# Attention products, value products and projections as 64x32 tiles on two row halves, with a new written order

## The chip, the cores and the metric

The kernel runs on one core of a Trainium2 chip. The metric is the device time of the program in microseconds. Engines are named as in the profile: PE (TensorE; PEld is its weight loads), ACT (ScalarE), DVE (VectorE), POOL (GpSimd) and SP (SyncE, which issues most DMAs).

## The reference

One input x (1 x 2048 x 512, bf16) goes through two attention layers of 32 heads of 16 each, and the two results are mixed by a gate:

```
g = sigmoid((x * gate_w).sum(-1, keepdims=True))

A:  q, k, v = heads of x @ wqkv
    pq = q @ w_phi ; pk = k @ w_phi                       (per head, 16 x 16)
    phi_q = [softmax(pq), softmax(-pq)] ; phi_k likewise
    kv = phi_k^T v ; z = sum over positions of phi_k
    o = (phi_q kv) / (phi_q z + 1e-6) ;  a = o @ wo

B:  q, k, v = heads of x @ wqkv
    p = softmax(q k^T / 4) ;  b = (p v) @ wo

out = g * a + (1 - g) * b
```

Layer B is the large part: 32 heads x 2048 x 2048 scores. Layer A is linear in the length.

## The kernel before, in words

**Blocks and tiles of layer B.** The 32 heads lie in four rows of eight (a row is the 128 partitions of a projected q or k). A block `b` of 32 is one row, one chunk of 512 queries and one parity, that is four heads: head `i` of the block sits in partitions 32i to 32i + 31 of `kT_B` (keys) and `qz` (queries; the other head of the same 32 partitions is zeroed in `qz`, of which there is one copy for each parity). A tile is (block, head i, key tile kt): 128 keys x 512 queries of scores, 64 tiles a block, 2048 in all.

**Scores.** `qk_mm` (line 1007) makes a tile with one matmul, contraction 32, 128 output columns: a row tile 32x128 of the array. Four heads have four row tiles, which may run side by side, each into a PSUM bank of its own. The order of heads over a block rotates.

**Two ways to an exponential.** 1272 tiles go in pairs (a slot) through ScalarE: `add_qk`, then `add_exp` (line 1131) exponentiates 128x1024 out of two neighbouring banks into `Ebuf`. The other 776 tiles (`DN` per block, in 202 groups of up to four) go through VectorE: `add_group` (line 1082) makes the tile (operation `dq`) and `D1` (line 1100, or 1090 for two tiles at once) turns scores into the bits of a bf16 exponential by an addition and a conversion to int16. GpSimd then adds constants to those bits (`shifted`, line 1076), twice, which gives two more terms of an approximation of the exponential.

**Value products.** `pv_mm` (line 1147) multiplies the exponentials of a tile with `vaug` (values and a column of ones): contraction 128, 32 output columns, so four heads are four column tiles 128x32 of the array, all adding into the one bank `psO` (`add_pv` for slots, `add_pvd` for the groups, whose tiles are multiplied three times, once for each term). At the end of a block VectorE copies `psO` out, and DMAs move the sums of the row of ones so that they can divide.

**Projections.** `columns` (line 765) does 128 x 512 outputs as four column tiles 128x32; `fill` (line 771) makes an operation of each contraction step, and `drain` the copy out of PSUM. The products with 128x128 or 128x64 weights (values, row sums of layer A, its kv and numerators) keep the whole array.

**What sets the order.** Nothing is scheduled on the chip. `Plan.add` records operations with what they read and write. `TABLE` holds, for each engine, the written order of the operations' numbers; `homes` gives the PSUM bank of each operation that opens one; `pairs` names the tiles that `D1` takes two at a time. `Plan.place` puts the lists together and adds what each operation waits for; `Plan.emit` (line 534) turns this into waits on one counting semaphore for each engine: each operation's last instruction raises its engine's count by one, and an engine waits until another's count is reached. An engine's own earlier operations are not waited for on PE. PE takes its instructions in the written order, so an operation that waits holds up all that stand behind it. PSUM has eight banks: six for slots, the same six and a seventh (`M`) for groups and fills, and one for `psO`.

```
def qk_mm(e, t, bank, half=None):
    b, i, kt = t
    cols = slice(0, NQ) if half is None else slice(256 * half, 256 * (half + 1))
    return e.matmul(bank, lhsT=kT_B[32 * i:32 * i + 32, ROW[b // 2] % 2, 128 * kt:128 * (kt + 1)],
                    rhs=qz[32 * i:32 * i + 32, b // 2 % 4, b % 2, cols], start=True, stop=True,
                    tile_position=(32 * i, 0))
```

## Time and profile before

| | |
|---|---|
| timed runs | 654.52 and 656.64 us, median 655.58 |
| profiled execution: span from first to last instruction | 653.1 us |
| busy in it: PE, PEld | 646.6, 229.7 us |
| busy in it: DVE, ACT, POOL | 615.8, 626.6, 420.4 us |
| TensorE clock granted | 1.000 |

The profile gives the span of the profiled execution; its own time lies beside it only as the timed runs do, 1.4 and 3.5 us above the span. PE's busy time runs from a matmul's start to its modelled end, and matmuls overlap, so 99% does not say that the array streams all the time: the distance from start to start does. The lines of `columns` (767), `qk_mm` (1010) and `pv_mm` (1152) are helpers' lines; they stand for many operations.

### The profile page before, as it was taken

To read this page: it belongs to the slowest core of one execution; us is meant where nothing else is said; L and a number is where in the kernel's file an instruction comes from. 1 tells how busy PE (TensorE), PEld (TensorE's weight loads), DVE (VectorE), ACT (ScalarE), POOL (GpSimd) and SP (SyncE) were. 2 spreads that over 40 slices of the span, in tenths; PEclk is the share of its full clock that TensorE was granted. 3 is DMA by queue.
4 is the path that set the end of the run, shared out by engine and by line. 5 is a ranking of instruction groups with operands and counts; after the bars stand their busy time and mean duration, and the time that the engine had idled before them with its cause. 6 is when DMAs were issued, how large, how long until landed. Compare 5 with 4: busy or idle time off the path is not lost.

```text
span 653.1 us, 20595 instructions
## 1 busy us (share of the span) xinstructions
PE 646.6 (99%) x8771; PEld 229.7 (35%) x8771; DVE 615.8 (94%) x1013; ACT 626.6 (96%) x710; POOL 420.4 (64%) x445
## 2 busy tenths in 40 slices
PE   9999999999999999999999999999999999999998
PEld 5332333433333333333333243333233234333333
DVE  6999899999999789999999999999999989999993
ACT  5999999899999999999999999989999999998996
POOL 7475567565657625676567777766875675577682
PEclk9999999999999999999999999999999999999999
DMA  7530101000010000100113331313201323035121
GB/s 131 116 90 20 24 13 29 11 11 21 10 29 10 19 12 11 26 13 6 29 39 92 63 99 48 78 34 82 52 23 49 85 53 96 33 82 111 29 58 59
DMA packets 67948, 30.95 MB, mean 47 GB/s; under 512 B 53208, under 2 KB 62808, under 8 KB 67856
## 3 DMA queue, kind: packets, MB, share of 16 engines
q1 hardware_dynamic: 65840, 28.82, 18.7%
q8 instruction: 69, 1.13, 0.7%
q10 hardware_dynamic: 1632, 0.79, 0.5%
q14 instruction: 23, 0.19, 0.1%
q0 software_dynamic: 384, 0.02, 0.1%
HBM read 7.87 MB, written 8.88 MB: 26 GB/s over the span
## 4 chain that ended last, share of the span: by engine, by line
PE 85%; ACT 10%; DVE 4%; issue 0%; DVEq 0%
PE psO L1152 32%; PE psS L1010 30%; PE psS L767 15%; ACT E_t L1131 10%; PE psS L1433 2%; PE psS L868 1%; PE psS L855 1%; DVE Tx_t L1100 1%; PE psS L1530 1%; DVE Ty_t L1100 1%; PE psS L1517 1%; PE psS L718 1%; DVE vA_t L1100 1%; DVE Wp_t L1100 0%; PE psS L1392 0%; PE psS L1473 0%
## 5 line engine op out<-in xcount | busy, mean ns | idle before, releaser
L1131 ACT ACTIVATE E_t<-psS 128x1024 bf16<-128x1024 f32 x633 | 592.4, 1059 | 15.3 <-PE psS L1010 14.5
L1010 PE MATMUL psS<-qz_t,kTB_t 32*128 32x512 bf16 (+1 forms) x2054 | 265.7, 384 | 2.0 <-ACT E_t L1120 0.6
L1100 DVE TENSOR_SCALAR Tx_t<-psS 128x512 int16<-128x512 f32 x268 | 175.3, 680 | 3.5 <-PE psS L1010 2.7
L1010 PEld LDWEIGHTS psS<-qz_t,kTB_t 32*128 32x128 bf16 x2054 | 72.9, 91 | 224.2 <-ACT E_t L1131 112.5
L1152 PE MATMUL psO<-E_t,vaug_t 128*32 128x512 bf16 x1272 | 124.4, 385 | 0.0
L1100 DVE TENSOR_SCALAR Ty_t<-psS 128x512 int16<-128x512 f32 x122 | 81.2, 683 | 5.5 <-PE psS L1010 5.2
L1076 POOL INT64_ADD vA_t<-vA_t x68 | 68.6, 1014 | 19.4 <-PE psO L1152 19.0
L1152 PE MATMUL psO<-vA_t,vaug_t 128*32 128x512 bf16 x534 | 53.1, 385 | 0.0
L1100 DVE TENSOR_SCALAR Tz_t<-psS 128x512 int16<-128x512 f32 x74 | 49.0, 681 | 2.5 <-PE psS L1010 2.0
L1076 POOL INT64_ADD Ty_t<-Ty_t x43 | 43.3, 1008 | 10.1 <-PE psO L1152 9.0
L1152 PEld LDWEIGHTS psO<-E_t,vaug_t 128*32 128x32 bf16 x1272 | 32.4, 95 | 42.8 <-issue 33.5
L1100 DVE TENSOR_SCALAR oT_t<-psS 128x512 int16<-128x512 f32 x66 | 43.9, 682 | 3.2 <-PE psS L1010 2.4
L1152 PE MATMUL psO<-Ty_t,vaug_t 128*32 128x512 bf16 (+1 forms) x450 | 45.9, 385 | 0.0
L1100 DVE TENSOR_SCALAR vA_t<-psS 128x512 int16<-128x512 f32 x66 | 44.1, 681 | 0.9 <-PE psS L1010 0.7
L1100 DVE TENSOR_SCALAR WAT_t<-psS 128x512 int16<-128x512 f32 x66 | 43.8, 680 | 0.4 <-PE psS L1010 0.4
L767 PE MATMUL psS<-Wp_t,xT_t 128*32 128x512 bf16 x512 | 41.2, 382 | 0.0
L767 PE MATMUL psS<-xT_t,WB_t 128*32 128x512 bf16 x480 | 39.1, 383 | 0.0
L1100 DVE TENSOR_SCALAR Wp_t<-psS 128x512 int16<-128x512 f32 x56 | 37.5, 681 | 0.5 <-PE psS L1010 0.5
L1076 POOL INT64_ADD phiQT_t<-Tx_t x19 | 19.3, 1015 | 22.9 <-DVE Tx_t L1100 20.7
L1076 POOL INT64_ADD Ty_t<-Tx_t x24 | 23.6, 984 | 15.6 <-DVE Tx_t L1100 15.5
L1076 POOL INT64_ADD WoB_t<-oT_t x19 | 18.9, 993 | 20.5 <-DVE oT_t L1100 18.5
L1076 POOL INT64_ADD WoA_t<-Tz_t x19 | 19.7, 1039 | 15.7 <-DVE Tz_t L1100 7.8
(166 smaller groups left out, 900.3 us busy)
## 6 DMA issues: line engine op xcount, KB each, us to landing
dpq<-EA_t SPq DMA_DIRECT2D x16, 256.0 KB, 2.3
Rb_t<-lr SPq DMA_DIRECT2D x120, 32.0 KB, 1.9
dpo<-kv_t SPq DMA_DIRECT2D x16, 128.0 KB, 1.8
qz_t<-qz_t SPq DMA_DIRECT2D x120, 16.0 KB, 1.8
Tf_t<-Tf_t SPq DMA_DIRECT2D x60, 32.0 KB, 2.0
WB_t<-in_B_wqkv_dram SPq DMA_DIRECT2D x3, 384.0 KB, 4.2
out_dram<-WvA_t SPq DMA_DIRECT2D x8, 128.0 KB, 2.0
out_dram<-WB_t SPq DMA_DIRECT2D x6, 128.0 KB, 1.9
```

The lines of the kernel that those rows point to most:

```text
L718: ins = e.matmul(psM, lhsT=ones[:, 0:128], rhs=ones, start=True, stop=True)
L767: ins = e.matmul(out[32 * i:32 * i + 32, :], lhsT=lhsT[:, 32 * i:32 * i + 32], rhs=rhs, start=start, stop=stop, tile_position=(0, 32 * i))
L855: mms = [lambda e, ap, i=i, t=t: e.matmul(ap[:, 128 * i:128 * (i + 1)], lhsT=xT[:, t, NQ * c + 128 * i:NQ * c + 128 * (i + 1)], rhs=W_B[:, ...
L868: mms = [lambda e, ap, i=i, t=t: e.matmul(ap[:, 256 * i:256 * (i + 1)], lhsT=xT[:, t, NQ * c + 128 * (2 * hf + i):NQ * c + 128 * (2 * hf + ...
L1010: return e.matmul(bank, lhsT=kT_B[32 * i:32 * i + 32, ROW[b // 2] % 2, 128 * kt:128 * (kt + 1)], rhs=qz[32 * i:32 * i + 32, b // 2 % 4, b ...
L1076: op = P.add("pool", P64 + W64 * size, d_prio(g["ts"][0]) - 5.0 + (0.0 if key == "s" else M_LATE), lambda e: e.int64_add(words(dst), words ...
L1100: ops.append(drain(f, mm, "dve", 0.70, d_prio(d), lambda e, ap, q=q: e.tensor_scalar(quarter(tb, q).bitcast(I16), ap, EXPB, 0.0, op0=ALU.a ...
L1131: op = P.add("act", EXP_OVH + 0.4267 * n, 0.0, lambda e: e.activation(Ebuf[:, j // 2 % EPAIRS, 512 * SZ[0] * (j % 2):512 * SZ[0] * (j % 2) ...
L1152: return e.matmul(psO[32 * i:32 * i + w, :], lhsT=vaug[:, kt, o:o + w], rhs=rhs, start=start, stop=stop, tile_position=(0, 32 * i), skip_g ...
L1433: mms = [lambda e, ap, n=n, f=f: e.matmul(ap[:, 64 * n:64 * n + 64].rearrange("p (s g j) -> p s g j", s=2, j=4), lhsT=ident[:], rhs=es[n][ ...
L1517: mms = [lambda e, ap, j=j, g=g: e.matmul(ap[:, 32 * j + 4 * g:32 * j + 4 * g + 4], lhsT=qT(g)[:, 128 * j:128 * (j + 1)], rhs=kzbd[:, g, 6 ...
L1530: mms = [lambda e, ap, g=g: e.matmul(ap[:, 64 * g:64 * g + 64], lhsT=qT(g)[:, 128 * j:128 * (j + 1)], rhs=kzbd[:, g, 0:64], start=True, st ...
```

## The change

- **Scores as 64x32 tiles.** A tile is made by four matmuls, each with contraction 64 (half of the partitions: heads 0 and 1 of a block lie in the lower half, 2 and 3 in the upper) and 32 output columns, all four into one bank. `qz` now holds four copies of a chunk, one for each (parity, head within the half), each zero but for its own 16 partitions; three chunks are kept in place of four, and `Qs` takes the projected queries, from which DMAs move 16 partitions each into place. `pmask` gets four more columns, filled by four small copies on GpSimd, for the first chunk.
- **Value products and split projections on halves.** `pv_mm` multiplies the lower and the upper 64 keys separately: two operations in place of one, each of four matmuls 64x32, both adding into `psO`. Where the side changes in PE's order on `psO`, the operation waits for the last one of the other side (`force`). A projection (`kind="col"`) does all its contraction steps on one half, then all on the other, in the same bank, with such a wait between; which half is first alternates.
- **A count for each half.** Half-array operations on the upper side raise a semaphore `pe_low` of their own; all other PE operations raise PE's as before.
- **Slots.** A slot holds the tiles of two heads with the same key tile (heads 0 and 1 or 2 and 3; in the first block 0 and 2 or 1 and 3). The two need no neighbouring banks: the exponential reads two banks at any distance. All seven banks but `psO` serve slots, groups and fills. `Ebuf` holds 10 slots of two tiles (before: 12).
- **Shares.** `DN` is a multiple of four in each block: 780 tiles in 195 groups on VectorE, 634 slots on ScalarE (before: 776 in 202 groups, 636 slots; 29 operations of two tiles at once in both).
- **Order.** `TABLE` is written anew for all engines. PE has 4938 operations (before: 3014), of which 4702 are half-array operations (2054 of scores, 1804 of values, 844 of projections), 218 use the whole array or 128x64, and 18 the old 128x32 form (`kind="all"`, last output tiles). POOL has 433 (before: 441), DVE 1021 after pairing (1013), ACT 681 (683), SP 259 as before. The planner's constants that set the old order are gone.

A stretch of PE's new order, in letters (q and d: scores for ScalarE and VectorE, p and t: value products of slots and groups, c: projections, f: whole array; a capital is the upper half):

```
qTqdPTdqTqPttQtQDDtQpQttDdTqPqdTTPqqPdtDtQpQDtppQtQtDTqTdTdqPTqTqfffffffff
```

```diff
-DN = (16, 24, 18, 26, 26, 26, 28, 20, 22, 24, 24, 18, 28, 24, 20, 26, 32, 22, 26, 26, 22, 26, 30, 26, 20, 22, 36, 20, 24, 24, 34, 16)
+DN = (16, 20, 24, 28, 24, 28, 20, 24, 24, 28, 24, 24, 24, 24, 24, 24, 28, 24, 28, 20, 28, 24, 28, 24, 24, 24, 28, 24, 24, 24, 24, 24)
...
+ESLOTS = 10
+QRING = 3
+HEADS = (2, 3, 0, 1)
 ENGINES = ("sp", "act", "pe", "dve", "pool")
+LANES = ENGINES + ("pe_low",)
...
+            if op.blk is not None:
+                op.open = op.blk not in ends
+                ends[op.blk] = op
+                if prev is None:
+                    op.banks = [output]
+                elif prev.side != op.side:
+                    op.force += (prev,)
+                prev = op
+            op.deps = op.deps + [d for d in op.force if d not in op.deps]
...
             for op in self.order[e]:
+                op.lane = LANES[5] if op.mode == "h" and op.side == 1 else e
+                op.below = counts[LANES[5]] if e == "pe" and op.mode != "h" else 0
                 if op.sem is None:
-                    counts[e] += 1
-                    op.count = counts[e]
+                    counts[op.lane] += 1
+                    op.count = counts[op.lane]
...
-                elif d.eng != op.eng or op.eng in ("act", "dve", "pool"):
...
+                elif d.eng != op.eng or op.eng in ("act", "dve", "pool") or d in op.force:
...
-    qz = sb([128, 4, 2, NQ], name="qz")
+    qz = sb([128, QRING, 4, NQ], name="qz")
+    Qs = sb([128, NQ], name="Qs")
...
-    def columns(e, out, lhsT, rhs, start, stop):
+    def columns(e, out, lhsT, rhs, start, stop, side=None):
+        o = 64 * (side or 0)
+        r = slice(0, 128) if side is None else slice(o, o + 64)
         for i in range(4):
...
+            ins = e.matmul(out[32 * i:32 * i + 32, :], lhsT=lhsT[r, 32 * i:32 * i + 32], rhs=rhs[r], start=start, stop=stop,
+                           tile_position=(o, 32 * i), skip_group_check=side is not None)
         return ins
...
+    def split(mms):
+        sides[0] += 1
+        a, last = sides[0] % 2, len(mms) - 1
+        return [(side, lambda e, ap, m=m, side=side, ends=(n == 0 and i == 0, n == 1 and i == last): m(e, ap, side, ends))
+                for n, side in enumerate((a, 1 - a)) for i, m in enumerate(mms)]
...
+            if prev is not None and prev.side != op.side:
+                op.force = (prev,)
...
+        drain(f, mm, "dve", 0.69, prio, lambda e, ap: e.tensor_single_scalar(Qs[:], ap, QSCALE, ALU.mult),
+              writes=["Qs"], name=f"Qe{r}.{qc}")
+        for par in range(2):
+            moves(f"q{par}{c}", lambda e, par=par: [e.dma_start(qz[o:o + 16, c, 2 * par + i % 2, :], Qs[o:o + 16, :])
+                                                    for i in range(4) for o in (32 * i + 16 * par,)], 4,
...
+    def qk_mm(e, t, bank, cols=slice(0, NQ)):
         b, i, kt = t
...
+        h = 64 * (i // 2)
+        for c in range(4):
+            ins = e.matmul(bank[32 * c:32 * c + 32, cols], lhsT=kT_B[h:h + 64, ROW[b // 2] % 2, 128 * kt + 32 * c:128 * kt + 32 * c + 32],
+                           rhs=qz[h:h + 64, b // 2 % QRING, b % 2 * 2 + i % 2, cols], start=True, stop=True,
+                           tile_position=(h, 32 * c))
+        return ins
...
+    def halves(op, t):
+        op.mode, op.side = "h", t[1] // 2
+        return op
...
+        def part(e, cols=slice(0, NQ)):
+            lo, hi = sorted(f.bank.index for f in fills)
+            return e.activation(Ebuf[:, j % ESLOTS, :, cols], two(psS[:])[:, lo:hi + 1:hi - lo, cols], ACTF.Exp, scale=ESCALE)
...
+    def pv_mm(e, op, work):
+        r = slice(64 * op.side, 64 * op.side + 64)
+        for (b, i, kt), rhs in work:
+            h = 8 * ROW[b // 2] + 2 * i + b % 2
+            o = VW * h - (16 if b % 2 and b < NB - 2 else 0)
+            w = VW if h % 8 == 7 and b >= NB - 2 else 32
+            ins = e.matmul(psO[32 * i:32 * i + w, :], lhsT=vaug[r, kt, o:o + w], rhs=rhs[r], start=op.open, stop=op.shut,
+                           tile_position=(64 * op.side, 32 * i), skip_group_check=True)
+        return ins
...
+    def add_sides(ts, rhs, reads, kind, name):
+        b = ts[0][0]
+        for side in range(2):
+            box = []
+            op = P.add("pe", 0.25, 0, lambda e, box=box: pv_mm(e, box[0], [(t, r()) for t, r in zip(ts, rhs)]),
+                       reads=reads + [("v", ROW[b // 2], c) for c in sorted({t[2] // 4 for t in ts})] + ["v1", "v2"],
+                       after=out_ops[b - 1] if b else (), name=f"{name}.{side}")
+            box.append(op)
+            op.kind, op.mode, op.side, op.blk = kind, "h", side, b
+            block_pv[b].append(op)
         return op
```

577 lines of the change are left out of this document (201 added, 376 removed), and 578 rows, old and new, of the table TABLE.

## The prediction

> **What bounds the kernel now.** I read the page's first part, then TensorE's timeline in a steady stretch, then the waits. (Times in the rows are us; the columns of a timeline are start, length, engine, line, operation, tiles, shape, count.)
>
> ```profile
> span 653.1 us, 20595 instructions
> PE 646.6 (99%) x8771; PEld 229.7 (35%) x8771; DVE 615.8 (94%) x1013; ACT 626.6 (96%) x710; POOL 420.4 (64%) x445
> ```
>
> Three engines are near full, so no single one can be relieved by much before the next binds. A busy TensorE need not be streaming, so its timeline comes next: attention products (L1010, four row tiles 32x128) against everything that runs as four column tiles 128x32 (L1152, L767).
>
> ```profile
> 402.02 0.39 PE L1010 MATMUL psS<-qz_t,kTB_t 32*128 32x512 bf16 x3
> 402.34 0.40 PE L1152 MATMUL psO<-Ty_t,vaug_t 128*32 128x512 bf16 x4
> 402.57 0.39 PE L1152 MATMUL psO<-E_t,vaug_t 128*32 128x512 bf16 x4
> 402.89 0.40 PE L1010 MATMUL psS<-qz_t,kTB_t 32*128 32x512 bf16 x4
> 403.21 0.40 PE L1152 MATMUL psO<-E_t,vaug_t 128*32 128x512 bf16 x4
> 403.44 0.39 PE L1152 MATMUL psO<-vA_t,vaug_t 128*32 128x512 bf16 x4
> ...
> 644.46 0.39 PE L1152 MATMUL psO<-Ty_t,vaug_t 128*32 128x512 bf16 x4
> 644.67 0.39 PE L1152 MATMUL psO<-E_t,vaug_t 128*32 128x512 bf16 x4
> 644.89 0.39 PE L1152 MATMUL psO<-vA_t,vaug_t 128*32 128x512 bf16 x4
> ```
>
> Read the starts, not the lengths. In one form a round of four follows the last after 0.216 (mean of 644.46 to 644.89). From row to column form and back it takes 0.32 (402.02 to 402.34, 402.57 to 402.89): a change of form costs 0.105, and the first round after it is 0.01 late. How often:
>
> ```profile
> PEld psO L1152 <- issue: 87.2, 373, 0.4
> PEld psS L767 <- issue: 22.3, 96, 0.4
> ```
>
> These are weight loads that waited for nothing but the drain on entering the column form: at least 469 entries, as many exits, 938 x 0.105 = 98 us of the span. ScalarE's waits for products are small beside it, and it runs back to back for long stretches (16.75/18 = 0.93 an exponential):
>
> ```profile
> ACT E_t L1131 <- PE psS L1010: 14.5, 34, 0.8
> ```
>
> ```profile
> 8.01 2.10 ACT L1120 ACTIVATE E_t<-psS 128x512 bf16<-128x512 f32 x4 [0.38 <-PE psS L1010]
> ...
> 629.21 16.75 ACT L1131 ACTIVATE E_t<-psS 128x1024 bf16<-128x1024 f32 x18
> ```
>
> **What the change takes away.** Products, value products and split projections share one form, 64x32, so the 938 changes go. In the new written order the matmuls in other forms (full array, 128x64, and the 128x32 of the last output tiles) stand in 61 stretches, of which the last has no exit. Against 98 us, 61 x 2 x 0.105 = 13 us of form changes stay.
>
> **What it adds: halves.** A product of one head and key tile becomes four matmuls on one row half (contraction 64, the other three heads of the half masked by zeros in qz), so a round holds two tiles where row form could hold four. Value products and projections keep eight matmuls per former four, each half as deep. Counting the new order: 2054 product operations, 1804 of values, 844 of projections, in all 4702 half-array operations of four matmuls. Paired perfectly that is 2351 rounds. Walking through the order as TensorE must, in sequence, and closing a round when a half comes up a second time (or a full-array operation comes between), I count 2573 rounds; in 444 one half stands unused. What a round of two halves costs no row shows. The lower bound is the 0.216 of one 128x32 round, the upper 0.432, two of them in series. I take 0.216, since row tiles already run side by side (402.89: four in one go). 2573 x 0.216 = 555.8.
>
> The feed must then deliver 16 instructions in 0.216. The densest stretch of the trace:
>
> ```profile
> 177.49 0.70 PE L1473 MATMUL psS<-vA_t,phiK_t 128*64 128x68 bf16 x32
> 178.12 0.39 PE L1010 MATMUL psS<-qz_t,kTB_t 32*128 32x512 bf16 x3
> ```
>
> 32 weight loads and 32 matmuls in 0.63 less the 0.105 exit: 16.4 ns a pair, so eight pairs take 0.131. The feed hides under the stream up to 27 ns a pair.
>
> **Waits it adds.** Both halves of a value product add into the one bank psO, so each change of side there (419 in the order) waits until the last matmul of the other side has landed, by TensorE waiting on its own count; every split projection has one such hand-over (92). Behind the waiting operation stand all later matmuls of both halves, behind those ScalarE and VectorE. No row shows TensorE waiting for itself. The nearest:
>
> ```profile
> 456.33 1.10 ACT L1131 ACTIVATE E_t<-psS 128x1024 bf16<-128x1024 f32 x1
> 457.48 0.18 PEld L1010 LDWEIGHTS psS<-qz_t,kTB_t 32*128 32x128 bf16 x5 [0.49 <-ACT E_t L1131]
> 457.49 0.61 PE L1010 MATMUL psS<-qz_t,kTB_t 32*128 32x512 bf16 x5
> 457.91 1.02 ACT L1131 ACTIVATE E_t<-psS 128x1024 bf16<-128x1024 f32 x1 [0.48 <-PE psS L1010]
> ```
>
> From a round's start to the engine it releases: 0.42 (457.49 to 457.91); TensorE itself reacts 0.05 after ScalarE's end (457.43 to 457.48). So I take 0.43 from start to start. Below it ends at 0.216, no wait at all; above I have only a bound by analogy, 0.43 plus a drain of 0.105, 0.53. In the order a hand-over on psO stands two rounds apart or more in 346 cases (0.432: free at 0.43), one or none in 73: 73 x (0.43 - 0.216) = 15.6 us. Of the projections' hand-overs none is nearer than two rounds. The Trainium skill, "TensorEngine Tiling (Array Packing)", Gotcha 1: PSUM Pressure, says that row tiles may not write one bank at once and that software has to keep them apart. By that these waits cannot be dropped; no run here shows it.
>
> **What stays.** Work in other forms, the answers for L1433, L868, L1530, L855, L1473, L1517, L1392 and L1377 over the span after the start (window, its length, TensorE's busy time):
>
> ```profile
> 8.00:653.00 645.00, 19.48 (x512) 16.55 (x512) 1.00 0.19 46
> 8.00:653.00 645.00, 9.25 (x64) 5.21 (x64) 1.00 0.19 46
> 8.00:653.00 645.00, 9.40 (x128) 7.26 (x128) 1.00 0.19 46
> 8.00:653.00 645.00, 6.20 (x128) 4.57 (x128) 1.00 0.19 46
> 8.00:653.00 645.00, 5.59 (x256) 4.69 (x256) 1.00 0.19 46
> 8.00:653.00 645.00, 3.96 (x128) 3.58 (x128) 1.00 0.19 46
> 8.00:653.00 645.00, 3.06 (x32) 1.81 (x32) 1.00 0.19 46
> 8.00:653.00 645.00, 2.35 (x64) 2.01 (x64) 1.00 0.19 46
> ```
>
> Together 59.3. How a visit begins and ends:
>
> ```profile
> 399.85 0.65 PE L1433 MATMUL psS<-EA_t,ident_t 128*128 128x64 bf16 x16
> 400.43 0.43 PE L1010 MATMUL psS<-qz_t,kTB_t 32*128 32x512 bf16 x3
> ```
>
> The products start 0.07 before the modelled end, so the exit lies inside the 59.3: less 61 x 0.07, plus 61 x 0.105 for the entries, 61.4. The 18 last output operations stay in the old column form: 18 x 0.216 = 3.9. Start and end:
>
> ```profile
> 7.69 0.29 PE L1010 MATMUL psS<-qz_t,kTB_t 32*128 32x256 bf16 x4
> ...
> 647.32 2.54 PE L767 MATMUL psS<-WoB_t,oT_t 128*32 128x512 bf16 x40
> ```
>
> 7.7 before the first product, and from the last round's end (649.9) to 653.1 another 3.2, plus 0.2 for that round's landing.
>
> **Sum for TensorE.** 7.7 + 555.8 + 15.6 + 61.4 + 3.9 + 3.4 = 647.8. Of the 15.6 a part falls on rounds whose second half I have already counted as unused, so it is 632 to 648 before any wait for banks; I expect most of the difference back as such waits and take 647.
>
> **Other edits.** The shares hardly move: 776 tiles on VectorE become 780, so 636 exponentials become 634. ScalarE saves 2 x 0.93 = 1.9. VectorE:
>
> ```profile
> L1100 DVE TENSOR_SCALAR Tx_t<-psS 128x512 int16<-128x512 f32 x268 | 175.3, 680 | 3.5 <-PE psS L1010 2.7
> ```
>
> ```profile
> 9.08 0.48 DVE L890 TENSOR_SCALAR qz_t<-psS,pmask_t 128x256 bf16<-128x256 f32 x1
> ```
>
> 4 x 0.68 for the tiles and 4 x 0.48 for the two extra masked copies of the first chunk: +4.6 us on 615.8, hidden while TensorE sets the end; if it doesn't, it is late by that. The first exponential still needs only ScalarE's own copy, which now waits for four small copies of pmask on GpSimd: 0 to +1. Banks for one exponential need no longer be neighbours, which can only free waits (0 to -5); a projection holds its bank through 4 + 4 rounds and a hand-over instead of four rounds, (5 x 0.216 - 0.2 = 0.9 us longer) x 92 = 83 of 7 x 650 bank-us, 0 to +3. The query moves lose one chained step on SP's queue and are filled four blocks ahead: nothing. POOL goes from 441 to 433 operations: nothing, at 64%.
>
> **The rivals.** *ScalarE sets the end.* If the halves mesh better than the order suggests, ScalarE loses its waits for products: 653.1 - 14.5 - 1.9 = 636.7. Start and end stay. VectorE would then be busy 620.4 of 636.7, 97%, and holds banks longer for it, so I leave a fifth of the waits: 639.6, time 642. For it: TensorE loses 85 us of form changes. Against it: the halved products give most of that back.
>
> *The hand-over is dearer.* At 0.53 instead of 0.43, the 235 + 39 hand-overs standing exactly two rounds apart and the 73 nearer ones each cost 0.1 more: 347 x 0.1 = 35 us, span 682, time 684: slower. It decides from 0.485 on (19 us). For it: no row shows such a wait. Against it: 457.49 to 457.91. The Trainium skill, "TensorE: Matmul & The Clock Gate", The cost: per-tile semaphore tail, gives a tail of 25 + 4.7 per tile + 26.3 ns per increment: an estimate of 45 ns more for eight tiles with two increments than for four with one. By that rule alone the span is 347 x 0.045 = 16 us longer and the time 665; no row here can show it, and I give it 1 in 10.
>
> *The halves don't overlap, or the feed is the bound.* At 30 ns a pair instead of 16.4 a round takes 0.24, 2573 x 0.024 = 62 us more, time 711. Against it stands the stretch at 177.49.
>
> **Numbers.** The profiled span is 653.1, the two timed runs 654.52 and 656.64, so 2.5 lies around it at the median. Forecast 647 + 2.5 = 649.5, chance 0.53, its own range 643 to 657 (632 to 648 of the sum with waits for banks, the edits' bounds of -5 to +5). ScalarE's bound at 642: 0.25. The dear hand-over 0.16: 0.1 for the tail at 665, 0.06 for 684. No overlap or a bound feed 0.06. The range, 638 to 672, takes in ScalarE's bound with no wait at all (639.2 less 1) and the tail's case with 7 us for banks. This kernel's measurement tells about 2% from no change, so the limits are 642.5 and 668.7. Faster: ScalarE's case, 0.25. Slower: 684, 711 and, with its bank waits, half of the tail's case: 0.06 + 0.06 + 0.05 = 0.17. The rest, 0.58, is no change.
>
> **What would show it.** Starts of L1010's and L1152's successors 0.216 apart, and two halves starting within some 10 ns, prove the round; a form change at only some 60 places; gaps of about 0.43 between the last value product of one side and the first of the other, the hand-over. ScalarE above 97% busy means the first rival; value products that start 0.5 or more after the other side's last, the second; rounds of 0.24, the third. I am wrong in kind if TensorE shows idle stretches that end on VectorE or ScalarE: then banks, not the array, set the pace.

## The result, and the profile after

The changed kernel takes 701.36 us, the median of two runs (699.85 and 702.86), against 655.58 for the kernel before: a ratio of 1.07 with a 95% interval of 1.063 to 1.077, so it is slower, by 46 us. The prediction was 649.5 with a range of 638 to 672; the time lies 29 us above the range.

The first part of the page of the changed kernel, with the chain of waits of its fourth part:

```profile
span 698.3 us, 43687 instructions
PE 680.6 (97%) x20236; PEld 343.1 (49%) x20236; DVE 630.7 (90%) x1021; ACT 631.5 (90%) x708; POOL 422.6 (61%) x437
...
PE 83%; ACT 6%; DVE 4%; DMA 4%; SPq 2%; issue 1%
```

ScalarE is busy about as long as before (631.5 against 626.6), so its idle time has grown from 26.5 to 66.8 us. VectorE's busy time is the union of its operations, of which fewer now overlap; its idle time has grown from 37 to 68. Transfers (DMA) and SyncE's queue (SPq) now stand in the chain of waits with 4% and 2%; the chain of before had neither.

The waits of the changed kernel (who waits and for what: us in all, times, longest), and one row of the kernel before that the prediction did not show:

```profile
PEld psS L1026 <- ACT E_t L1122: 57.2, 193, 0.7
PEld psO L1148 <- PE psO L1148: 44.4, 146, 0.6
ACT E_t L1122 <- PE psS L1026: 42.5, 55, 4.1
...
PE psS L804 <- DMA dpq<-EA_t: 4.1, 3, 2.8
```

```profile
PEld psS L1010 <- ACT E_t L1131: 112.5, 288, 0.6
```

ScalarE's waits for products went from 14.5 to 42.5 us, and single ones last up to 4.1. The second row is the new hand-over on psO. The row of before looks like 112.5 us of waiting for ScalarE to give banks back, but it is not. It makes 0.39 us a time, and a weight load on the same line that waited for nothing but the change of form stands nearly as long (first row below, 0.34). With ScalarE and VectorE reading 64 of 512 columns (two runs described below), the row of before keeps three quarters of it (second row), while the same wait of the changed kernel nearly goes, from 57.2 to 2.4 (third row):

```profile
PEld psS L1010 <- issue: 27.5, 80, 0.4
PEld psS L1010 <- ACT E_t L1139: 85.4, 208, 0.6
PEld psS L1026 <- ACT E_t L1127: 2.4, 6, 0.7
```

In the trace of before, ScalarE had given the bank back a median of 0.18 us before such a weight load began; in the changed kernel it is 0.04. So the 112.5 us are for the most part the drain of the change of form under ScalarE's name, and the 57.2 us of the changed kernel are true waits.

The groups of the exponentials by line and shape, after and before (busy, mean ns of one, idle before them and its cause):

```profile
L1122 ACT ACTIVATE E_t<-psS 128x1024 bf16<-128x1024 f32 x631 | 595.3, 1037 | 44.6 <-PE psS L1026 40.6 <-PE psO L1148 2.2
```

```profile
L1131 ACT ACTIVATE E_t<-psS 128x1024 bf16<-128x1024 f32 x633 | 592.4, 1059 | 15.3 <-PE psS L1010 14.5
```

**TensorE's new rounds.** The timeline of a stretch with projections (start, length, engine, line, operation, tiles, shape, count):

```profile
300.15 0.39 PE L804 MATMUL psS<-Wp_t,xT_t 64*32 64x512 bf16 x4
300.16 0.39 PE L804 MATMUL psS<-WvA_t,xT_t 64*32 64x512 bf16 x4
300.37 0.39 PE L804 MATMUL psS<-Wp_t,xT_t 64*32 64x512 bf16 x4
300.38 0.39 PE L804 MATMUL psS<-WvA_t,xT_t 64*32 64x512 bf16 x4
300.58 0.39 PE L804 MATMUL psS<-Wp_t,xT_t 64*32 64x512 bf16 x4
300.59 0.39 PE L1148 MATMUL psO<-WoB_t,vaug_t 64*32 64x512 bf16 x4
...
301.10 0.10 PEld L1148 LDWEIGHTS psO<-E_t,vaug_t 64*32 64x32 bf16 x4 [0.18 <-PE psO L1148]
301.10 0.40 PE L1148 MATMUL psO<-E_t,vaug_t 64*32 64x512 bf16 x4
```

Each half starts an operation every 0.215, and the two halves run side by side, 0.01 apart. The value product at 300.59 is of the upper half, the one at 301.10 of the lower: a hand-over of 0.51 here. Where the weight load stood waiting for the other side, the median is 0.47 from start to start and the least 0.46; over all 419 changes of side on psO the median is 0.505, since some of them wait for other things too.

**Where TensorE's time went.** From the starts of all 4702 half-array operations (each streams 0.216) I added up, from 8 us to the last round, how long both halves, one half or none streamed, and set that beside the terms of the prediction:

| us | predicted | changed kernel |
|---|---|---|
| both halves stream | 459.9 | 428.7 |
| one half alone | 96 (444 rounds) | 154.0 |
| full array, form changes, last outputs | 65.3 | 60.5 |
| nothing streams, no visit of another form | 15.6 | 43.7 |
| start and end | 11.1 | 11.4 |
| sum | 647.8 | 698.3 |

The first row predicted is 2573 less 444 rounds of 0.216. So the work was as forecast, but the halves mesh worse (one half alone for 58 us more, which costs half of that) and stand still together 28 us longer. The count does not say whether TensorE's own list or the engines behind it cause this; the runs with short drains do.

**Where on the way it was lost.** The time between the ends of ScalarE's exponentials of the same number, from both traces:

| exponentials | before | after | difference |
|---|---|---|---|
| start to 0 | 8.6 | 11.9 | 3.3 |
| 0 to 160 | 159.9 | 163.8 | 3.9 |
| 160 to 320 | 159.3 | 177.0 | 17.7 |
| 320 to 400 | 80.5 | 84.4 | 3.9 |
| 400 to 480 | 80.2 | 94.0 | 13.8 |
| 480 to 635 | 154.7 | 154.4 | -0.3 |
| 635 to the end | 9.9 | 12.8 | 2.9 |

Three of these stages (160 to 320, 400 to 480, 520 to 600), by busy time of the engines in the two traces (length, then PE, PEld, DVE, ACT, POOL with their instructions; clock; DMA share; GB/s):

```profile
175.70:352.70 177.00, 174.97 (x5348) 90.27 (x5344) 164.27 (x257) 162.62 (x186) 104.21 (x111) 1.00 0.08 20
437.10:531.10 94.00, 88.69 (x2680) 44.38 (x2673) 82.80 (x134) 81.61 (x93) 56.70 (x55) 0.98 0.28 57
570.50:653.20 82.70, 80.98 (x2392) 39.22 (x2392) 76.68 (x120) 75.69 (x81) 51.10 (x50) 0.98 0.30 61
```

```profile
168.50:327.80 159.30, 159.23 (x2296) 57.95 (x2292) 150.16 (x238) 158.00 (x181) 95.39 (x102) 1.00 0.08 16
408.30:488.50 80.20, 80.03 (x1031) 25.69 (x1023) 80.04 (x128) 77.45 (x87) 58.44 (x61) 1.00 0.22 55
526.60:610.40 83.80, 82.97 (x1157) 29.52 (x1150) 81.87 (x135) 79.00 (x88) 56.08 (x54) 1.00 0.31 71
```

In the first stage ScalarE was idle 1.3 us before and is idle 14.4 now; in the last the two kernels are alike. So in that stage halves and hand-overs run attention as fast as the old forms did, though it also holds fewer projection operations than before (40 against 57, in full ones). Most of the loss falls where projections and the feature-map layer come in between. The new order also puts more of them there: 46.5 projection operations (in full ones) against 32 between exponentials 240 and 320, 62 against 44 between 400 and 480, which at 0.216 is 7 us of the 31.

### The profile page after: what moved, and what is told of

Same layout as the page of the kernel before. It is cut to its first block, busy times and chain, and to the rows that moved or that the text cites. A ratio compares the mean times of both kernels' runs of the same rounds, so it can differ in the third digit from the quotient of the medians.

```text
span 698.3 us, 43687 instructions
## 1 busy us (share of the span) xinstructions
PE 680.6 (97%) x20236; PEld 343.1 (49%) x20236; DVE 630.7 (90%) x1021; ACT 631.5 (90%) x708; POOL 422.6 (61%) x437
## 4 chain that ended last, share of the span: by engine, by line
PE 83%; ACT 6%; DVE 4%; DMA 4%; SPq 2%; issue 1%
PE psS L1026 33%; PE psO L1148 30%; PE psS L804 13%; ACT E_t L1122 6%; DMA dpq<-EA_t 2%; PE psS L1379 2%; SPq L1451 1%; PE psS L919 1%; PE psS L906 1%; PE psS L1419 1%; DMA phiK_t<-in_A_x_dram 1%; PE psS L1476 1%; DVE Tx_t L1091 1%; DVE Ty_t L1099 0%; SPq L958 0%
## 5 line engine op out<-in xcount | busy, mean ns | idle before, releaser
L1122 ACT ACTIVATE E_t<-psS 128x1024 bf16<-128x1024 f32 (+1 forms) x637 | 598.4, 1033 | 46.5 <-PE psS L1026 42.5
L1026 PE MATMUL psS<-qz_t,kTB_t 64*32 64x512 bf16 (+1 forms) x8216 | 521.7, 381 | 3.3 <-ACT E_t L1122 0.9
L1026 PEld LDWEIGHTS psS<-qz_t,kTB_t 64*32 64x32 bf16 x8216 | 164.3, 90 | 170.3 <-ACT E_t L1122 57.2
L1148 PE MATMUL psO<-E_t,vaug_t 64*32 64x512 bf16 (+1 forms) x2536 | 225.5, 380 | 1.5 <-DVE Tf_t L1194 0.8
L1148 PE MATMUL psO<-vA_t,vaug_t 64*32 64x512 bf16 x1048 | 95.3, 380 | 0.3
L1148 PE MATMUL psO<-Ty_t,vaug_t 64*32 64x512 bf16 x888 | 85.6, 380 | 0.1
L1148 PEld LDWEIGHTS psO<-E_t,vaug_t 64*32 64x32 bf16 (+1 forms) x2536 | 62.4, 91 | 40.3 <-PE psO L1148 14.9
L804 PE MATMUL psS<-Wp_t,xT_t 64*32 64x512 bf16 x1024 | 70.2, 383 | 4.2 <-DMA dpq<-EA_t 4.1
L804 PE MATMUL psS<-xT_t,WB_t 64*32 64x512 bf16 x960 | 72.1, 378 | 0.0
L1148 PE MATMUL psO<-Tx_t,vaug_t 64*32 64x512 bf16 x576 | 54.7, 378 | 0.0
```

The source lines that it names most:

```text
L804: ins = e.matmul(out[32 * i:32 * i + 32, :], lhsT=lhsT[r, 32 * i:32 * i + 32], rhs=rhs[r], start=start, stop=stop, tile_position=(o, 32 * ...
L1026: ins = e.matmul(bank[32 * c:32 * c + 32, cols], lhsT=kT_B[h:h + 64, ROW[b // 2] % 2, 128 * kt + 32 * c:128 * kt + 32 * c + 32], rhs=qz[h: ...
L1122: return e.activation(Ebuf[:, j % ESLOTS, :, cols], two(psS[:])[:, lo:hi + 1:hi - lo, cols], ACTF.Exp, scale=ESCALE)
L1148: ins = e.matmul(psO[32 * i:32 * i + w, :], lhsT=vaug[r, kt, o:o + w], rhs=rhs[r], start=op.open, stop=op.shut, tile_position=(64 * op.sid ...
```

## The experiments

Theory one was the prediction's: TensorE's sum is right, and what is lost are waits for banks and for the engines behind it. Theory two: TensorE's own list has become dearer. Every time below stands beside runs of the kernel before on the same chip, 654.2 to 656.7 us. The changed kernel itself was not run there; its two runs lie 3 us apart, and nearly every time below is of one run, so a difference of 3 us or less says nothing.

**Short drains.** In both kernels ScalarE and VectorE read 64 of 512 columns:

```diff
-        def part(e, cols=slice(0, NQ)):
+        def part(e, cols=slice(0, NQ if j < ESLOTS else 64)):
...
+        w = NQ if g["t"] not in seen else 64
...
-                quarter(tb, q).bitcast(I16), ap, EXPB, 0.0, op0=ALU.add, op1=ALU.max),
+                quarter(tb, q)[:, 0:w].bitcast(I16), ap[:, 0:w], EXPB, 0.0, op0=ALU.add, op1=ALU.max),
```

> The changed kernel with the engines behind TensorE made light: every exponential on ScalarE after the first ten, and every tile on VectorE after the first group of a buffer, works on 64 of its 512 columns (the other columns keep what an earlier use left there), so banks come free at once. Order, waits, banks and all of TensorE's work stay. Theory one, TensorE's own time was summed rightly at 632 to 648 and the lost 50 us are waits for banks and for exponentials: 640 to 652. Theory two, TensorE alone is dearer than the sum (hand-overs, lateness of one half behind the other, the feed): 680 or more. Between 655 and 680 both have a part, in proportion.

> The same lightening in the kernel before: exponentials and VectorE's tiles on 64 of 512 columns, all else as it was. Both theories: TensorE had little slack before (ScalarE's waits for products were 14.5 us and the array was busy 99%), so about 635, at least 630 and no more than 650. The difference to the lightened changed kernel is what the change does to TensorE alone: theory one about +10, theory two +45 or more.

> The changed kernel with only the exponentials on ScalarE cut to 64 of 512 columns; VectorE's tiles stay whole. If waits for ScalarE's banks and for its exponentials are what is lost (theory one in its first form), as low as with both cut, 640 to 655. If VectorE's tiles hold the banks, it stays near 690. If TensorE alone is dearer, 680 or more here too.

> The changed kernel with only VectorE's tiles cut to 64 of 512 columns; the exponentials stay whole. If VectorE holds the banks: 640 to 660. If ScalarE is what TensorE waits for: 680 to 695, near the changed kernel's 701. If TensorE alone is dearer: 685 or more.

Measured: 687.25 for the changed kernel, 641.34 for the one before; with only the exponentials short 695.97, with only VectorE's tiles short 697.77. The pages of the two, the changed kernel first:

```profile
span 685.6 us, 43687 instructions
...
PE 660.0 (96%) x20236; PEld 354.6 (52%) x20236; DVE 327.3 (48%) x1021; ACT 219.5 (32%) x708; POOL 422.4 (62%) x437
```

```profile
span 639.5 us, 20595 instructions
...
PE 632.8 (99%) x8771; PEld 217.4 (34%) x8771; DVE 317.6 (50%) x1013; ACT 218.9 (34%) x710; POOL 418.9 (66%) x445
```

Both kernels gain 14 us, and the difference between them stays 46. With ScalarE a third and VectorE half busy, the changed kernel's TensorE still needs 685, as theory two expected (680 or more): theory one falls. The same count as above gives 439.6 us with both halves streaming, 130.1 with one and 104.7 with none (visits of other forms included), 674.4 in all, against 459.9, 96 and 80.9 predicted. The two runs with one engine short show a second trait of this kernel: 5 us from the one engine, 4 from the other, but 14 from both.

**Transfers and hand-overs.** The first two runs below let no TensorE operation wait for a transfer of the feature-map layer; the last two lay the banks out over six, and then give the empty bank to the value sums of one half (`op.side` 1, the upper half in the words of this document; the expectation calls it the lower; the second diff):

```diff
-                     after=va_free if qk else pw_ops[st - 2:st - 1] if st > 1 else [])
+                     after=va_free if qk else [])
...
-        moves(f"pw{b}", lambda e: e.dma_start(dpq[n, 128 * j:128 * (j + 1), :], EA[:, b, :]), 1, [("EA", b)],
+        op = moves(f"pw{b}", lambda e: e.dma_start(dpq[n, 128 * j:128 * (j + 1), :], xT[:, 0, 0:1024]), 1, xk(0) + xk(1),
...
-        ls = [oAT[:, t, 128 * tile:128 * (tile + 1)] for t in range(KT)] if with_a else []
+        ls = [xT[:, 0, 128 * tile:128 * (tile + 1)] for t in range(KT)] if with_a else []
```

```diff
-            ins = e.matmul(psO[32 * i:32 * i + w, :], lhsT=vaug[r, kt, o:o + w], rhs=rhs[r], start=op.open, stop=op.shut,
+            to = psS[:, 512 * 0:512 * 1] if op.side else psO
+            ins = e.matmul(to[32 * i:32 * i + w, :], lhsT=vaug[r, kt, o:o + w], rhs=rhs[r], start=op.open, stop=op.shut,
...
-                elif prev.side != op.side:
-                    op.force += (prev,)
```

> The changed kernel, drains whole again, in which no TensorE operation of the feature-map layer waits for a transfer: its staging writes go out from an unchanging piece of xT instead of EA and oA, and the denominators, the numerators and the output projections read xT where they read the transposed copies (so that layer's part of the output is left out; the transfers themselves, their number, size and queues stay). In the trace of the changed kernel 12 us of the span have TensorE streaming nothing while the next operation waits for such a transfer. If these waits are lost time: 688 to 692. If they fall where ScalarE and VectorE are behind anyway: 698 or more.

> The same in the lightened kernel (exponentials and VectorE's tiles on 64 of 512 columns, 687 us): its trace has 14 us of such waits. If the waits are TensorE's only loss beside the sum: 640 to 650. If hand-overs and the halves' own order are the loss: 671 to 676.

> The lightened kernel with the products, projections and the rest laid out over six banks instead of seven (bank 0 stays empty after the start; two of TensorE's operations stand a few places earlier than before, the rest of every order as it was). It is the base for the next run. Every theory: with drains this short six banks do, so 687 to 700.

> The same as the run with six banks, but the value products of the lower row half add into the empty bank, so no change of side on psO waits for the other side (what the lower half summed is left out of the output; the projections keep their 92 hand-overs). My prediction's price, 73 near hand-overs at 0.21: 15 us less than with six banks. If hand-overs stop both halves and nearly all of the 419 cost: 35 to 50 us less. If the halves' order or the feed is the loss: within 8 us.

Measured: 700.08 without the transfer waits, 681.24 with short drains besides, which neither expectation for that run had. In the whole kernel these waits cost nothing that the spread of the runs would show (between exponentials 400 and 480 the stage falls from 94.0 to 89.5, and the next one, to 520, gives 3.1 back); in the light one 6 us. Six banks: 711.87, and without hand-overs on psO 697.75.

```profile
span 710.3 us, 43672 instructions
```

```profile
span 696.1 us, 43755 instructions
```

So hand-overs on psO are worth 14.1 us there, close to the 15.6 of the prediction. The base came out above its range (687 to 700): one bank less costs 25 us even with exponentials of 0.28 us. That had not been expected by either theory.

**TensorE light, and two parts undone.**

```diff
-            f, mm = fill(0, [lambda e, ap, t=d["t"]: qk_mm(e, t, ap)], [kkey(ROW[b // 2], kt), q_key(d["t"])], name=f"dq{b}.{kt}.{i}",
+            f, mm = fill(0, [lambda e, ap, t=d["t"], w=NQ if g["n"] < 5 else 256: qk_mm(e, t, ap, slice(0, w))], [kkey(ROW[b // 2], kt), q_key(d["t"])], name=f"dq{b}.{kt}.{i}",
...
-            ins = e.matmul(psO[32 * i:32 * i + w, :], lhsT=vaug[r, kt, o:o + w], rhs=rhs[r], start=op.open, stop=op.shut,
+            n = NQ if b < 1 else 256
+            ins = e.matmul(psO[32 * i:32 * i + w, 0:n], lhsT=vaug[r, kt, o:o + w], rhs=rhs[r, 0:n], start=op.open, stop=op.shut,
```

```diff
-                op.lane = LANES[5] if op.mode == "h" and op.side == 1 else e
+                op.lane = e
```

```diff
-        for c in range(4):
-            ins = e.matmul(bank[32 * c:32 * c + 32, cols], lhsT=kT_B[h:h + 64, ROW[b // 2] % 2, 128 * kt + 32 * c:128 * kt + 32 * c + 32],
-                           rhs=qz[h:h + 64, b // 2 % QRING, b % 2 * 2 + i % 2, cols], start=True, stop=True,
-                           tile_position=(h, 32 * c))
+        ins = e.matmul(bank[:, cols], lhsT=kT_B[32 * i:32 * i + 32, ROW[b // 2] % 2, 128 * kt:128 * kt + 128],
+                       rhs=qz[32 * i:32 * i + 32, b // 2 % QRING, b % 2 * 2 + i % 2, cols], start=True, stop=True,
+                       tile_position=(32 * i, 0))
```

> The mirror of the lightened kernels: the changed kernel with TensorE made light. Products after the first twenty exponentials and the first five groups of VectorE's tiles, and value products after the first block, stream 256 of their 512 columns (the rest of each bank keeps older values, so the output is not attention any more); ScalarE, VectorE, GpSimd, all waits and all orders stay whole. Theory one, TensorE's own time is what is lost: with about 200 us of streaming gone the other engines' floor shows, 640 to 655. Theory two, the loss is the chain through all engines (a bank is filled, lands 0.42 later, is read, and comes free) in the new order, in which TensorE's width matters little: 672 to 685.

> The same lightening of TensorE in the kernel before. Its ScalarE was idle 15 us for products and TensorE had 14 us of slack with short drains, so both theories: 636 to 648. The difference to the changed kernel with a light TensorE is what the new order and its longer hops cost the other engines: theory one 0 to 10, theory two 30 or more.

> One part of the change undone: both row halves count on one semaphore again (the waits on the other half's count become waits on the same count). If TensorE's operations complete strictly in the written order, as the trace of the changed kernel shows for all 4938, the second semaphore buys nothing: 696 to 706. If it does let one half's results out ahead of the other's: 710 or more.

> Another part undone: the attention products go back to one 32x128 row tile of one matmul each (same result), while value products and projections stay as halves, in the new written order, which goes 2764 times from a product to something else or back. With 0.105 us for each change of form and no overlap across it: 2764 x (0.216 + 0.105) plus some 60 for the rest, 930 to 1000. If a row tile of one half and a column tile of the other run side by side, as two halves do: 700 to 760.

Measured: 699.5 and 672.25 with half the stream, but at a granted clock of 0.939 and 0.84, so the expectations, which both miss, can't be judged by them. One semaphore for both halves: 697.91, so the second semaphore buys nothing. Products in row form within the new order: 1954.06. Its timeline and a stretch of its span (the last three figures are clock, DMA share, GB/s):

```profile
899.42 0.62 PE L1147 MATMUL psO<-E_t,vaug_t 64*32 64x512 bf16 x4
899.97 0.61 PE L1025 MATMUL psS<-qz_t,kTB_t 32*128 32x512 bf16 x2
900.50 0.62 PE L1147 MATMUL psO<-oT_t,vaug_t 64*32 64x512 bf16 x4
901.05 0.61 PE L1025 MATMUL psS<-qz_t,kTB_t 32*128 32x512 bf16 x2
...
901.60 0.62 PE L804 MATMUL psS<-Wp_t,xT_t 64*32 64x512 bf16 x4
...
902.00 0.64 PE L804 MATMUL psS<-Wp_t,xT_t 64*32 64x512 bf16 x4
...
902.43 1.07 PE L804 MATMUL psS<-Wp_t,xT_t 64*32 64x512 bf16 x8
```

```profile
100.00:1000.00 900.00, 899.92 (x6743) 203.51 (x6741) 311.90 (x453) 318.31 (x332) 186.10 (x194) 0.52 0.03 6
```

Across a change of form the halves do not run side by side (the starts are 0.54 apart), and the clock stays at half, so the time is twice what I had expected. What it would be at full clock no run shows: 1010 (1954 x 0.517) is too low, since a change of form takes 0.54 from start to start here and 0.32 in the kernel before, 0.59 of it. The expectation of 930 to 1000 was low in another term too: the 2764 changes take 1473 us of the trace, and the rest, put at 60, some 480. The new order is not usable without the new form; the new form in the old order was not run.

**The written order.** TensorE's list was laid anew by a replay of the measured trace, first for short drains, then with ScalarE's and VectorE's lists for whole ones. Only the lists of operation numbers and the banks' list change, here the first line of TensorE's that does in the second run:

```diff
-        118, 119, 1171, 1172, 1068, 1061, 1059, 1066, 1175, 1174, 267, 268, 1070, 1062, 1180, 1179, 1072, 1060, 1177, 1182, 121, 1169, 122, 1183,
+        118, 119, 1171, 1172, 1068, 1061, 1059, 1066, 1175, 1174, 1062, 267, 268, 1177, 1070, 1179, 1180, 1169, 1060, 1182, 121, 122, 1185, 1183,
```

> The lightened changed kernel (exponentials and VectorE's tiles on 64 of 512 columns, 687 us) with TensorE's written order laid anew: each operation keeps its half, its bank and its neighbours in that bank; about 4400 of 4938 stand some places earlier or later, so that the halves are filled more evenly and fewer operations queue behind one that waits (396 to 400 changes of side on psO instead of 419, so hand-overs are hardly fewer). The order came from a replay of the measured trace, which puts this kernel at 635 to 645. If what TensorE lost is how waits and halves follow one another in the written order: 640 to 655. If it is the rate of the rounds, the feed or a longer hand-over: 675 or more.

> The changed kernel, drains whole, with the written orders of TensorE, ScalarE and VectorE laid anew in the same way for whole drains (3956 operations of TensorE moved, 7 of ScalarE, 222 of VectorE). If the order of TensorE alone is what the change lost: 655 to 665. If ScalarE, VectorE and the seven banks hold the chain near that time whatever TensorE's order is: 685 to 693, 8 to 13 under the changed kernel.

Measured: 674.1 with short drains, 13 us less, and 718.65 with whole ones (ratio to before 1.100, interval 1.095 to 1.105), 17 us more than the changed kernel. The order moves the time by such amounts, but my replay is no guide to it: it missed by some 30 us both times. So neither expectation holds; that a better order exists is shown for short drains only.

**A quarter off TensorE's streams** (384 of 512 columns), which keeps the clock at 0.988 in the changed kernel and 0.995 in the one before:

> The changed kernel with TensorE a quarter lighter instead of half: 384 of 512 columns in the products after the first twenty exponentials and the first five groups, and in the value products after the first block (so again not attention), to see the effect with less of the clock loss that the half-light kernels showed (0.939 and 0.84 granted). A quarter of some 500 us of half-array streaming goes. If TensorE's width bounds the changed kernel: 655 to 670. If the chain through all engines does, with TensorE's part in it the landing and the written order rather than its width: 690 to 701.

> The same quarter taken from the kernel before. If its TensorE's width is its bound: 635 to 645. If its other engines hold it near its time (ScalarE busy 96%): 648 to 658.

Measured: 695.88 for the changed kernel, 654.36 for the one before. TensorE's busy time, changed kernel first:

```profile
PE 653.7 (94%) x20236; PEld 325.7 (47%) x20236; DVE 625.9 (90%) x1021; ACT 626.9 (90%) x708; POOL 423.1 (61%) x437
```

```profile
PE 617.2 (95%) x8771; PEld 240.9 (37%) x8771; DVE 616.0 (94%) x1013; ACT 624.8 (96%) x710; POOL 420.2 (64%) x445
```

Neither kernel is bound by the width of TensorE's streams: a quarter less gives 5 us in the one and nothing in the other, as the second expectation of each had it. (The lost clock, 0.988 against 0.995, may hide up to 5 us more in the changed kernel, an estimate: 0.7% of 695.) The chain of waits of the kernel before, as it was and with a quarter less:

```profile
PE 85%; ACT 10%; DVE 4%; issue 0%; DVEq 0%
```

```profile
ACT 73%; PE 12%; DVE 12%; DMA 1%; issue 1%; SPq 1%; DVEq 0%
```

So in the kernel before ScalarE holds the same time as soon as TensorE is lighter, and its waits for products stay as they were (15.8 us, 14.5 without the edit).

**Banks, and both reliefs at once.** A projection holds its bank 5.47 us on average, against 3.33 before (from its first start to the end of its drain); I had taken 0.9 longer. All holds together make 3993 bank-us of 7 x 695, against 3727 of 7 x 650: the same share, 0.82, in both.

```diff
             on, mms = zip(*split(mms))
+            skip = len(mms) // 2
...
+            on, mms = on[skip:], mms[skip:]
```

> The changed kernel with only the second half of each of its 92 split projections: the first four (or, for the parts, as many as the first side has) operations leave the order, and the bank is taken at the first one of the second side (so queries, keys, features and outputs lack half their sum; every transfer, drain and other wait stays). In the trace a projection holds its bank 5.47 us, against 3.33 in the kernel before: 504 of 3993 bank-us, 266 more in all than before. The width of TensorE's streams is worth little (5 us for a quarter of it). If the banks' time is what the change lost: some 230 bank-us less, over 7 banks that are 0.82 in use, 40 us: 655 to 668. If it is the landing and the order of waits of products and values: 688 to 697.

> Both reliefs at once in the changed kernel: exponentials and VectorE's tiles on 64 of 512 columns, and products and value products on 384 of 512 (so neither attention nor its exponentials are whole). Alone the first gave 14 us and the second 5. If TensorE's list and the lists of ScalarE and VectorE each hold the time near 690 by themselves and hand their delays to each other, the two together give far more than the sum: a replay of the lightened trace with narrower streams gives 53 us less than without, so 625 to 645. If something else, say GpSimd's shifts or the transfers, holds the time: 675 or more.

Measured: 691.55 with half the projections, 10 us less where the banks' theory wanted 33 or more, so the time for which projections hold banks is not the main cause (the run also takes half of the projections' streams away). Both reliefs at once: 665.73, at a clock of 0.966. That is 36 us for short drains and narrow streams together, where alone they gave 14 and 5. It falls between the two expectations: two near floors that hand delays to each other fit the 36, but they do not explain all, and the lost clock hides how much. The kernel before was not run with both, so how much of the 666 is due to the change stays open.

## Why the prediction was wrong, step by step

**"What bounds the kernel now" was the step that failed first; it is why nothing could be won.** It rightly said that no engine could be relieved by much before the next binds, and then summed TensorE alone, with ScalarE's bound at 639.6 in a rival. Taking a quarter of TensorE's streams away left the old kernel at 654.36, with a span of 652.5 and ScalarE as 73% of its chain of waits. So in the old order ScalarE's bound is near 652.5, 13 above what the rival had; the 14.5 us of its waits for products, which the rival took off, do not go when TensorE is lighter. The drains of 98 us that the change removes are on TensorE's path, but ScalarE's stands beside it at nearly the same time.

**The sum for TensorE, 647.8, failed second; it is where the 46 us lie.** With short drains the new list takes 685.6 and the old one 639.5, as far apart as the whole kernels. The single prices held. A round of two halves is 0.216, and the feed of twice as many instructions hides (issue is 1% of the chain of waits). The 61 visits of other forms are there, and entering one costs 0.31 from start to start, 0.09 more than a round. What failed is the walk through the order, a model in which each operation finds its banks and its data ready. With short drains, where ScalarE and VectorE hardly hold TensorE up, the halves mesh worse than in the walk by 14 us (439.6 + 130.1 against 459.9 + 96) and nothing streams for 24 us more (104.7 against 80.9); these make the 38 us from 647.8 to 685.6. In the whole kernel "in 444 one half stands unused" became 154 us, or 713 rounds' worth, and "15.6" for hand-overs became 43.7 us of standstill of all kinds.

**The hand-over** was priced at 0.43 and is 0.47; its 15.6 us for psO stand beside 14.1 measured with six banks. That the two are so near is in part luck: by the prediction's own count the 0.04 more on 235 + 73 hand-overs would make it some 28. The tail by which the Trainium skill ("TensorE: Matmul & The Clock Gate", The cost: per-tile semaphore tail) made it 45 ns dearer is near the 40 ns found. But the 0.43 was taken from a wait of ScalarE for TensorE, so this does not test that rule, and the 16 us that I had hung on it are not what the kernel lost. My rival of a dearer hand-over, which was to decide from 0.485 on, is not what happened, and neither are the other two: ScalarE is 90% busy, not above 97%, and rounds are 0.216, not 0.24. None of the rivals was a loss spread over all engines.

**"I am wrong in kind if TensorE shows idle stretches that end on VectorE or ScalarE"** came true in the letter: 57.2 us of true waits on ScalarE. It was no test of what sets the pace, since with those waits at 2.4 us the kernel gains 14 us and stays 46 behind. That banks are not what lost the time by themselves is shown by the short drains, where the difference of 46 us stays, and by half the projections, where it shrinks by 10.

**Other edits.** The start costs 3.3 us, not 0 to 1: the first exponentials, which began at 8.01 before, begin here at 11.28:

```profile
11.28 1.65 ACT L1122 ACTIVATE E_t<-psS 128x512 bf16<-128x512 f32 x3 [1.75 <-PE psS L1026]
```

That banks of one exponential need no longer be neighbours gains nothing here: in the order that was laid out all 634 pairs are neighbours. Projections hold banks 2.1 us longer, not 0.9. "Nothing" for SP's queue holds in the whole kernel as far as the run without transfer waits shows: 700.08 against 701.36.

**What stays open.** Shown parts, in the kernel with short drains: 14 us for hand-overs on psO (with six banks; the sum had them at 15.6), 6 for transfers (the sum had none) and 13 for the order. They were tried one at a time, so they need not add up. In the whole kernel only 10 (half the projections), 5 (streams) and 14 (drains) could be moved one at a time. What makes products come late between exponentials 160 and 480 is not settled, but two things narrow it. ScalarE's waits do not depend on the width of TensorE's streams: before its wide exponentials it was idle 44.6 us in the changed kernel and is idle 46.0 with a quarter less:

```profile
L1122 ACT ACTIVATE E_t<-psS 128x1024 bf16<-128x1024 f32 x631 | 592.3, 1083 | 46.0 <-PE psS L1026 42.2 <-PE psO L1149 1.7 <-PE psS L804 0.8
```

They mostly stand before the same exponentials, with much the same lengths, so they come with the written order. The other is a trait that was seen but not tried alone, the full-array work in longer visits: 17 stretches of other forms last over 1 us (28 us in all, the longest 3.2) against 10 before (11 us, the longest 1.3). Such a visit in the timeline:

```profile
241.29 0.39 PE L1026 MATMUL psS<-qz_t,kTB_t 64*32 64x512 bf16 x4
241.61 1.92 PE L919 MATMUL psS<-WB_t,xT_t 128*128 128x256 bf16 x16
243.37 1.11 PE L1379 MATMUL psS<-phiK_t,ident_t 128*128 128x64 bf16 x32
244.41 0.40 PE L1026 MATMUL psS<-qz_t,kTB_t 64*32 64x512 bf16 x4
```

No product starts for 3.1 us, and ScalarE then stands for 2.0 (1.9 with a quarter off the streams, 2.0 with half the projections). Of the 46.5 us that ScalarE waits before all its exponentials, 15.5 end during one of the 17 long visits or within 1.3 us after it; in the kernel before it is 0.9 of 15.7, with 10 such visits. So about half of the 31 us by which these waits grew goes with the long visits; that shorter ones would win it back was not tried.

## What to carry to other kernels

Where three engines are 94 to 99% busy, the longest sum is not the time: before costing a saving on one engine, make its work a quarter lighter and see whether the kernel moves at all. A wait that the profile puts down to an engine is shown to be that engine's only when it goes as the engine is made light: 112.5 us became 85.4 here in one kernel, and 57.2 became 2.4 in the other. The new tile form brought waits of its own and an order of its own, so what counted was not the drains it removed but how long both halves streamed at once, and that is read from starts, not from a busy share that stays at 97%. When relieving each engine alone gives little and relieving two gives more than their sum, look for stages in which they starve each other rather than for one culprit.

## What the runs showed of the hardware that was not expected

**Starts pass each other, completions don't.** Three operations in their order of start:

```profile
127.63 0.39 PE L1026 MATMUL psS<-qz_t,kTB_t 64*32 64x512 bf16 x4
127.68 0.39 PE L1148 MATMUL psO<-E_t,vaug_t 64*32 64x512 bf16 x4
...
127.90 0.39 PE L1148 MATMUL psO<-Ty_t,vaug_t 64*32 64x512 bf16 x4
```

The product at 127.63, of the upper half, is written behind both value products, which are of the lower half. It starts ahead of them, but its semaphore counts only at 128.38, 0.06 after that of the last value product and 0.36 after its own modelled end. In the trace 381 operations start ahead of an earlier one of the other half, by up to 0.585; of 4938 operations none counts ahead of an earlier one, and 474 count more than 0.1 after their own end. So a second semaphore has nothing to tell earlier, and one does as well as two (697.91). The Trainium skill, "TensorE: Matmul & The Clock Gate", Part 3: Packing small matmuls, says that matmuls start and end in program order; for ends this trace agrees, for starts on two row halves it does not.

**The price of a form change hardly follows the clock.** At half clock a change takes (901.05 - 899.42) / 3 = 0.54 from start to start where the same form takes (902.43 - 901.60) / 2 = 0.415: the change costs 0.13, against 0.105 at full clock in the kernel before, where 0.21 would be in proportion. The column tiles are not the same in the two (64x32 here, 128x32 there).

**A busy TensorE can lose its clock.** With products in row form TensorE is busy 100% by the profile's page and is granted 0.52; with half-width streams 0.94 and 0.84 at 88 and 91% busy; with a quarter less 0.988 and 0.995 at 94 and 95%. The Trainium skill, "TensorE: Matmul & The Clock Gate", Part 1: The HAM clock gate, says that the gate watches how busy the array has been. No run here measures that directly; what they show is that the busy share of the profile's page does not tell the clock. An experiment that makes TensorE light must therefore be read with its clock beside it.
